# Software pipelining of the head pairs and bf16 masks in a sparse-attention and expert-layer kernel

## The chip, the cores and the metric

The kernel runs on one core of one Trainium2 chip. The metric is device time in microseconds (us) of that core. Engines are named as in the profile: PE (TensorE matmuls), PEld (TensorE weight loads, which overlap PE), DVE (VectorE), ACT (ScalarE), POOL (GpSimd) and SP (the queue that issues transfers).

A single run can be labelled slow when it lies over 1.5% above the fastest of its kernel. Ratios below are the mean time of one kernel's fast runs over the mean of the other's fast runs in the same rounds on the same chip, so a ratio is not quite the ratio of the medians that stand beside it.

## The reference

There are 4 batches of 8 heads with 768 positions of 64 elements. Heads 0, 2 and 6 of each batch are causal. The other five "stream": a query sees the first 4 positions and the last 64. The attention output, as 3072 tokens of 512 elements, goes through an expert layer.

```python
scores = (1.0 / np.sqrt(D)) * np.matmul(q, k.transpose(0, 1, 3, 2))
# causal = rel >= 0;  stream = causal & (is_sink | rel < window)
scores = np.where(mask[None], scores, -1e9)
a = np.exp(scores - np.max(scores, axis=-1, keepdims=True))
a = a / (np.sum(a, axis=-1, keepdims=True) + 1e-09)
x = np.matmul(a, v)            # then (B, H, S, D) -> (B*S, H*D)
h = x @ w_in                   # 512 -> 2048
out = (h / (1.0 + np.exp(-beta * h))) @ w_out   # 2048 -> 512
```

## The kernel before

The first 46 us load and prepare masks and weights. Then come 16 head pairs, two heads (128 rows of data) at a time. The expert stage ends the kernel. For one pair the kernel transposes q and k on TensorE, forms transposed scores block by block for the blocks that the mask leaves, takes the exponential on ScalarE, multiplies by a 0/1 mask on VectorE, and multiplies by V, which carries a column of ones, so that column 64 of the result is the sum of the weights.

```python
# ... pools of the attention stage (bufs = buffers that rotate)
ain bufs=2; aes bufs=3; psp (score PSUM) bufs=4; pou (sum PSUM) bufs=2; ptr (transpose PSUM) bufs=2
for b in range(B):
    for hp in range(0, H, 2):
        # ... load q2, k2, v2; cast to bf16
        for t in range(T):                                  # T = 6
            tpq = ptr.tile([128, 128], BF16, name="tpt")
            nc.tensor.transpose(tpq, q2b[:, t, :, :], ident_bf)
            nc.any.tensor_copy(out=QT2[:, t * 128:(t + 1) * 128], in_=tpq)
            # ... the same for k
        for hh in range(2):
            # ... plan: list of (key block, first and last query block)
            es_all = aes.tile([128, 8, 512], BF16, name="es_all")
            for idx, (kj, ca, cb) in enumerate(plan):
                sp = psp.tile([128, 512], F32, name="sp")
                nc.tensor.matmul(sp[:, 0:w], KT2[po:po + D, ...], QT2[po:po + D, ...])
                nc.scalar.activation(out=esd, in_=sp[:, 0:w], func=Exp, scale=scale)
                # causal head: the diagonal block *= Mc
                # streaming head: esd *= Mstr0[...] (key block 0) or Mstrd[:, 0:w]; masks are fp32
            for qi in range(T):
                pout = pou.tile([128, D + 1], F32, name="pout")
                for j, (idx, kj, cc) in enumerate(contrib):
                    nc.tensor.matmul(pout, es_all[:, idx, ...], V_ext[:, kj, hh, :], ...)
                nc.vector.reciprocal(rec, pout[:, D:D + 1])
                nc.vector.tensor_scalar(out=oqd2[:, qi, hh, :], in0=pout[:, 0:D], scalar1=rec, ...)
        for qi in range(T):
            # ... transpose oqd2 on TensorE (a "tpt" tile again), copy into xT
# ... expert stage: 768 matmuls of 512 columns
```

The order of instructions within each engine is fixed when the program is built, by a list scheduler. `nc.any` lets it choose the engine of a copy. An engine can therefore stand in front of an instruction whose input is not ready: in the kernel before, TensorE stood 36.4 us in front of weighted sums (below).

The softmax here doesn't subtract the row's maximum and nothing guards it: scores larger than these inputs give would overflow.

## Time and profile before

| | before |
|---|---|
| median of 5 runs | 466.07 us (465.95 to 467.4) |
| profiled span | 465.0 us |
| loading, attention, expert stage | to 46, to about 290, to the end |
| time of one causal+streaming pair | 15.75 us |

These lines of the page of the kernel before give each engine's busy time, share of the span and instruction count, then, per engine, the busy share in tenths for 40 equal slices of the span. PEclk is the granted clock of TensorE.

```profile
PE 349.1 (75%) x1844; PEld 160.2 (34%) x1844; DVE 189.0 (41%) x771; ACT 210.8 (45%) x567; POOL 5.4 (1%) x19
...
PE   0000866786677667866786678899999999999996
...
DVE  1094557856767677567756775300000000000000
ACT  0000654565456445644564456552615335272541
...
PEclk9999999999999999999999999999999999999999
```

In the attention, slices 5 to 25, PE shows 6 to 8, DVE mostly 5 to 7, ACT 4 to 6. No engine is full. Soon after, PE is at 9: the expert stage is at TensorE's limit.

This line of the windows view of the kernel before covers attention. After the window and its length, it gives the busy us of PE, PEld, DVE, ACT and POOL with instruction counts, then the granted clock, the DMA share and GB/s.

```profile
46.00:290.00 244.00, 179.18 (x1054) 83.63 (x1055) 165.37 (x715) 137.34 (x443) 0.00 (x0) 1.00 0.35 73
```

Of 244 us PE is busy 179 (73%), DVE 165 (68%), ACT 137 (56%).

These are groups of instructions of the kernel before, each with one shape: line, engine, operation, tiles, shapes and count, then busy us and the mean ns of one, then the engine's idle time before them and what ended it.

```profile
L305 PE MATMUL op<-w_out_sb,gT 128*128 128x512 bf16 x384 | 83.9, 379 | 0.0
L253 PE MATMUL pout<-V_ext,es_all 128*128 128x65 bf16 x552 | 65.7, 241 | 37.5 <-DVE oqd L262 36.4
...
L212 PE MATMUL sp<-QT,KT 64*128 64x512 bf16 x56 | 33.3, 616 | 0.0
...
L241 DVE TENSOR_TENSOR es_all<-es_all,Mstrd 128x256 bf16<-128x256 bf16 x80 | 29.3, 416 | 0.0
...
L229 DVE TENSOR_TENSOR es_all<-es_all,Mc 128x128 bf16<-128x128 bf16 x72 | 17.4, 283 | 0.2
...
L236 DVE TENSOR_TENSOR es_all<-es_all,Mstr 128x512 bf16<-128x512 bf16 x20 | 13.6, 682 | 0.1
```

A 512-column matmul takes 379 ns in the expert stage (L305) and 616 ns as a score matmul (L212). A mask multiply on 256 columns (L241) takes 416 ns.

These lines of the table of waits of the kernel before say who waited for whom, for how many us in total, how often, and the longest wait.

```profile
PEld L253 <- DVE oqd L262: 54.1, 80, 1.9
...
PE pout L253 <- DVE oqd L262: 36.4, 53, 1.8
```

The weighted sums (pout) wait for the scaling (oqd), because the two PSUM banks of the sums come free only when the scaling has read them.

These are pieces of the chain of waits in one pair of the kernel before (start us, length us, what was on the chain).

```profile
98.37 1.60 PE sp L212 x5
...
103.63 0.73 PE pout L253 x11
...
104.39 0.17 DVE rec L261
104.56 0.32 DVE es_all L236
104.88 0.39 DVE oqd L262 x2
105.27 1.54 DVE es_all L241 x5
106.80 0.14 DVE rec L261 x2
106.95 0.26 DVE oqd L262
```

The chain goes through five score matmuls on TensorE, later through eleven sums, and then leaves TensorE: from 104.39 to 107.2 us it lies on VectorE's reciprocals, masks and scalings, and TensorE waits. This line of the page sums the whole chain by engine.

```profile
PE 63%; DVE 23%; issue 6%; ACT 5%; POOL 1%; DMA 1%; SPq 0%; POOLq 0%; ACTq 0%; DVEq 0%
```

VectorE has 23% of the chain though it is never full.

### The profile page before, as it was taken

What the parts mean: (1) busy time and instruction counts of PE and PEld (TensorE: products, weight loads), DVE (VectorE), ACT (ScalarE), POOL (GpSimd) and SP (SyncE); (2) the same over time, 40 slices, a digit from 0 to 9 for tenths busy, and PEclk for the clock granted to TensorE, in tenths of its full rate; (3) what the DMA queues carried; (4) which work ended last, traced back from release to release, by engine and by line L of the source; (5) the groups of instructions that cost most, each with busy time, mean ns of one, the idle gap of its engine ahead of it and who ended that gap; (6) DMA issues with size and microseconds to landing.
All of it is one profiled execution on the core that took longest, in us unless ns stands there. A gap on an engine that the chain in (4) does not pass through costs nothing.

```text
span 465.0 us, 5398 instructions
## 1 busy us (share of the span) xinstructions
PE 349.1 (75%) x1844; PEld 160.2 (34%) x1844; DVE 189.0 (41%) x771; ACT 210.8 (45%) x567; POOL 5.4 (1%) x19
## 2 busy tenths in 40 slices
PE   0000866786677667866786678899999999999996
PEld 0000333333333333333333333344444444444442
DVE  1094557856767677567756775300000000000000
ACT  0000654565456445644564456552615335272541
POOL 2100000000000000000000000000000000000000
PEclk9999999999999999999999999999999999999999
DMA  7916993452332333414310000002011010101101
GB/s 268 397 58 123 200 173 82 89 117 48 83 75 68 87 83 69 103 38 100 68 34 2 0 2 0 1 0 90 1 45 47 23 69 0 68 24 45 47 23 68
DMA packets 83404, 33.91 MB, mean 73 GB/s; under 512 B 77745, under 2 KB 77745, under 8 KB 82865
## 3 DMA queue, kind: packets, MB, share of 16 engines
q1 hardware_dynamic: 83378, 33.58, 28.3%
q8 instruction: 14, 0.23, 0.2%
q14 instruction: 12, 0.10, 0.1%
HBM read 27.28 MB, written 6.29 MB: 72 GB/s over the span
## 4 chain that ended last, share of the span: by engine, by line
PE 63%; DVE 23%; issue 6%; ACT 5%; POOL 1%; DMA 1%; SPq 0%; POOLq 0%; ACTq 0%; DVEq 0%
PE op L305 18%; PE sp L212 12%; PE pout L253 8%; DVE es_all L241 6%; PE tpt L185 5%; DVE oqd L262 5%; ACT KT L186 3%; DVE rec L261 3%; DVE es_all L236 2%; DVE w_in_sb L118 2%; DVE V_ext L175 2%; DVE w_out_sb L126 1%; PE tpt L273 1%; ACT xT L274 1%; DMA q<-in_q_dram 1%
## 5 line engine op out<-in xcount | busy, mean ns | idle before, releaser
L253 PE MATMUL pout<-V_ext,es_all 128*128 128x65 bf16 x552 | 65.7, 241 | 37.5 <-DVE oqd L262 36.4
L220 ACT ACTIVATE es_all<-sp 128x256 bf16<-128x256 f32 (+3 forms) x236 | 85.2, 429 | 18.4 <-PE sp L212 14.0
L305 PE MATMUL op<-w_out_sb,gT 128*128 128x512 bf16 x384 | 83.9, 379 | 0.0
L212 PE MATMUL sp<-QT,KT 64*128 64x256 bf16 (+3 forms) x236 | 78.8, 439 | 0.0
L253 PEld LDWEIGHTS <-es_all 128*128 128x128 bf16 x552 | 38.7, 119 | 86.7 <-DVE oqd L262 54.1
L182 PE MATMUL tpt<-idb,q2b 128*128 128x128 bf16 x96 | 28.5, 297 | 45.8 <-DVE q2b L171 45.5
L274 ACT COPY xT<-tpt 128x128 bf16<-128x128 bf16 x93 | 24.8, 266 | 71.7 <-PE tpt L273 68.4
L290 PEld LDWEIGHTS <-w_in_sb 128*128 128x128 bf16 x384 | 37.9, 99 | 47.2 <-issue 3.9
L305 PEld LDWEIGHTS <-gT 128*128 128x128 bf16 x384 | 37.6, 98 | 45.2
L262 DVE TENSOR_SCALAR oqd<-pout,rec 128x64 bf16<-128x64 f32 x192 | 48.9, 278 | 2.0
L313 ACT COPY osb<-op 128x512 f32<-128x512 f32 x24 | 14.1, 586 | 69.0 <-PE op L305 69.0
L261 DVE RECIPROCAL rec<-pout 128x1 f32<-128x1 f32 x192 | 29.8, 164 | 30.5 <-PE pout L253 27.9
L185 PE MATMUL tpt<-idb,k2b 128*128 128x128 bf16 x96 | 25.9, 270 | 19.0 <-ACT KT L186 11.3
L182 PEld LDWEIGHTS <-q2b 128*128 128x128 bf16 x96 | 10.3, 108 | 70.8 <-issue 70.8
L273 PE MATMUL tpt<-idb,oqd 128*128 128x128 bf16 x96 | 27.3, 289 | 8.2 <-DVE V_ext L176 6.6
L241 DVE TENSOR_TENSOR es_all<-es_all,Mstrd 128x256 bf16<-128x256 bf16 (+1 forms) x100 | 33.3, 390 | 0.0
L212 PEld LDWEIGHTS <-KT 64*128 64x128 bf16 x236 | 22.9, 117 | 27.2 <-issue 17.3
L186 ACT COPY KT<-tpt 128x128 bf16<-128x128 bf16 x79 | 21.1, 267 | 22.2 <-PE tpt L185 22.2
L183 ACT ACT_TABLE_LOAD x1 | 1.3, 1283 | 45.8 <-PE tpt L182 45.8
L236 DVE TENSOR_TENSOR es_all<-es_all,Mstr 128x512 bf16<-128x512 bf16 (+1 forms) x40 | 21.6, 546 | 0.3 <-ACT es_all L220 0.2
L183 DVE COPY QT<-tpt 128x128 bf16<-128x128 bf16 x59 | 13.1, 222 | 17.6 <-PE tpt L182 17.6
L229 DVE TENSOR_TENSOR es_all<-es_all,Mc 128x128 bf16<-128x128 bf16 x72 | 17.4, 283 | 0.2
(231 smaller groups left out, 251.5 us busy)
## 6 DMA issues: line engine op xcount, KB each, us to landing
q<-in_q_dram SPq DMA_DIRECT2D x32, 192.0 KB, 3.3
k<-in_k_dram SPq DMA_DIRECT2D x32, 192.0 KB, 3.4
v<-in_v_dram SPq DMA_DIRECT2D x32, 192.0 KB, 3.0
out_dram<-osb SPq DMA_DIRECT2D x24, 256.0 KB, 2.0
w_in_f<-in_moe_w_in_dram SPq DMA_DIRECT2D x1, 4096.0 KB, 13.2
w_out_f<-in_moe_w_out_dram SPq DMA_DIRECT2D x1, 4096.0 KB, 22.7
beta_row<-in_moe_beta_dram SPq DMA_DIRECT2D x1, 8.0 KB
beta_p<-in_moe_beta_dram SPq DMA_DIRECT2D x1, 8.0 KB, 3.4
```

Source lines behind the costliest of these rows:

```text
L182: nc.tensor.transpose(tpq, q2b[:, t, :, :], ident_bf)
L185: nc.tensor.transpose(tpk, k2b[:, t, :, :], ident_bf)
L186: nc.any.tensor_copy(out=KT2[:, t * 128:(t + 1) * 128], in_=tpk)
L212: nc.tensor.matmul(sp[:, 0:w], KT2[po:po + D, kj * 128:(kj + 1) * 128], QT2[po:po + D, ca * 128:(cb + 1) * 128], start=True, stop=True,)
L220: nc.scalar.activation(out=esd, in_=sp[:, 0:w], func=mybir.ActivationFunctionType.Exp, scale=scale,)
L241: nc.vector.tensor_mul(esd, esd, Mstrd[:, 0:w],)
L253: nc.tensor.matmul(pout, es_all[:, idx, cc * 128:(cc + 1) * 128], V_ext[:, kj, hh, :], start=(j == 0), stop=(j == nci - 1),)
L261: nc.vector.reciprocal(rec, pout[:, D:D + 1])
L262: nc.vector.tensor_scalar(out=oqd2[:, qi, hh, :], in0=pout[:, 0:D], scalar1=rec, scalar2=None, op0=mybir.AluOpType.mult,)
L273: nc.tensor.transpose(tpo, oqd2[:, qi, :, :], ident_bf)
L290: nc.tensor.matmul(hp_, w_in_sb[:, mo, fi * 128:(fi + 1) * 128], xT[:, mo, n0:n0 + NCHUNK], start=(mo == 0), stop=(mo == MO - 1),)
L305: nc.tensor.matmul(op, gT[:, fi, ns * 128:(ns + 1) * 128], w_out_sb[:, fi, :], start=(fi == 0), stop=(fi == FO - 1),)
```

## The change

Its intent is to let the phase of a pair that hangs on VectorE run beside the next pair's transposes and scores, and to make the mask multiplies cheaper. The diff, cut to its core (re-indentation left out):

```diff
+    Mc_b = consts.tile([128, 128], BF16, name="Mc_b")
+    nc.vector.tensor_copy(out=Mc_b, in_=Mc)
+    # ... the same for Mstr0_b (768 columns) and Mstrd_b (256)
@@ pools
-         tc.tile_pool(name="a_in", bufs=2) as ain, \
-         tc.tile_pool(name="a_es", bufs=3) as aes, \
+         tc.tile_pool(name="a_in", bufs=3) as ain, \
+         tc.tile_pool(name="a_es", bufs=2) as aes, \
-         tc.tile_pool(name="a_ps_sp", bufs=4, ...) as psp, \
-         tc.tile_pool(name="a_ps_ou", bufs=2, ...) as pou, \
+         tc.tile_pool(name="a_ps_sp", bufs=3, ...) as psp, \
+         tc.tile_pool(name="a_ps_ou", bufs=3, ...) as pou, \
@@ a pair is split in two
+        def part1(b, hp):   # loads, casts, transposes, scores, exp, masks
+            es_all = aes.tile([128, 2, 8, 512], BF16, name="es_all")   # both heads
-                                    Mc,
+                                Mc_b,
-                                    Mstr0[:, ca * 128:(cb + 1) * 128],
+                                esd, esd, Mstr0_b[:, ca * 128:(cb + 1) * 128]
-                                    esd, esd, Mstrd[:, 0:w],
+                            nc.vector.tensor_mul(esd, esd, Mstrd_b[:, 0:w])
+        def part2(st):      # weighted sums, scaling, output transposes
+        for (b, hp) in pairs:
+            st = part1(b, hp)
+            if pend is not None:
+                part2(pend)
+            pend = st
+        part2(pend)
```

## The prediction

It was written before the changed kernel was built or run.

> **What bounds it now.** The activity rows split the 465.0 us span into loading to 46 us, attention from 46 to about 290, and the expert stage, where TensorE runs at its limit (768 matmuls, 215 ns apart) and nothing changes. So the 244 us of attention count: 16 head pairs, 15.75 us for a causal+streaming pair and 14.8 us for the all-streaming one (start to start of the same burst in the timeline). There TensorE is busy 73%, VectorE 68%, ScalarE 56%: none is full. The chain of waits shows three phases in series per pair: about 4 us of q/k transposes, a ping-pong with the copies out of two PSUM tiles; about 6 us of score matmuls paced by TensorE; about 5.5 us in which VectorE's mask multiplies, reciprocals and scalings hold up the weighted sums (in the table of waits TensorE waits 36 us on the scaling).
>
> TensorE runs at half rate throughout attention: the 512-column score matmul takes 616 ns, the 65-column one 241, while 512 columns take 379 ns in the expert stage. The Trainium skill, "TensorE: Matmul & The Clock Gate", section "Single matmul latency", gives (219+N)/1.2 cold, (398+N)/2.4 warm: 609, 237 and 379 ns; the trace agrees. The granted-clock row (1.00) does not show this gate.
>
> **What the change does.**
> 1. bf16 masks. Mask multiplies take 416 ns (256 wide), 682 (512), 283 (128)[...]. The skill's "VectorE: DVE Perf Modes", "The perf-mode tier table", puts an all-bf16 two-input op at twice that rate. Estimate: 133 ns saved per 256 columns, 80x133 + 20x267 + 20x133 + 92x67 ns = 25 us of VectorE. About 10 us lies on today's chain. Three mask casts are added where VectorE idles 11.6 us: free.
> 2. Software pipelining: transposes, scores and exps of pair i+1 precede the weighted sums of pair i, so the VectorE-bound phase overlaps the next pair's other phases. Nothing is removed.
> 3. Buffers: scores 4 to 3 PSUM banks, sums 2 to 3. Exp needs about 0.36 us per 256-wide tile, the round trip over three banks about 0.9: no new limit.
>
> **The sum.** Per pair afterwards: TensorE, cold, 4.8 (scores) + 2.7 (sums) + 18 transposes at about 0.18 = 10.7 us; VectorE about 9; ScalarE about 8.6. TensorE binds. With 10% lost to fixed instruction orders that mismatch real times: 11.7 us. 16 x 11.7 + 6 us (ends unoverlapped) = 193 us instead of 244: total about 413 us.
>
> **Predicted: 413 us, 8 in 10 between 388 and 440.** Faster by over 2%: 0.9; within 2%: 0.07; slower: 0.03.
>
> **What would show the steps.** Right: 11 to 12.5 us per pair; waits of the sums on the scaling from 36 us to under 12; sums of pair i between score matmuls of pair i+1 in the timeline; 256-wide mask multiply near 280 ns, 512-wide near 415; expert stage unchanged near 171 us; TensorE over 85% busy in attention. Wrong: mask multiplies keep their durations; pairs stay above 14 us.
>
> **What would make it wrong.** Down: if TensorE becomes dense enough to leave its cold state, score matmuls fall to about 380 ns (512 wide) and VectorE at 9 to 10 us a pair binds: about 385 to 390 (I give this 35%). Up: the two transpose tiles are shared by q/k and output transposes; if their order couples the pairs, the overlap is partial: about 435. Or the changed PSUM banks delay the expert stage by a few us.

## The result, and the profile after

| | before | after |
|---|---|---|
| median | 466.16 us (15 runs) | 409.22 us (9 runs, 407.41 to 410.13) |
| ratio of fast runs | | 0.8772 (95%: 0.8757 to 0.8788) |
| profiled span | 465.0 us | 407.4 us |
| attention | 46 to about 290 us | 46 to about 235 us |
| one causal+streaming pair, from first score matmul to first score matmul | 15.75 us | about 12.0 us (10.9 for two streaming heads) |
| copies out of the transpose tiles on ACT / DVE | 209 / 79 | 258 / 30 |

The result is correct and 57 us faster. The lines of the page of the kernel after that answer to those above:

```profile
PE 339.7 (83%) x1844; PEld 158.9 (39%) x1844; DVE 154.1 (38%) x725; ACT 219.0 (54%) x616; POOL 5.5 (1%) x19
...
PE   0000398899898999898999999999999999999996
...
DVE  0268267767777767766667710000000000000000
ACT  0000477777778777877777665164262461541731
...
PEclk9999999999999999999999999999999999999999
```

From the sixth slice on PE reads 8 or 9, through attention and expert stage alike; the long stretch of 6 to 8 is gone. The windows view of the kernel after, for attention:

```profile
46.00:235.00 189.00, 171.06 (x1073) 82.97 (x1073) 133.34 (x685) 145.29 (x491) 0.00 (x0) 1.00 0.47 94
```

Of 189 us PE is busy 171 (90%), DVE 133 (71%), ACT 145 (77%). PE's busy time fell by 8 us only, so most of the gain is idle time that was filled: 65 us idle before, 18 after. Per pair (one sixteenth) that is 10.7 us of PE, 8.3 of DVE and 9.1 of ACT.

The groups of the kernel after, each with one shape:

```profile
L324 PE MATMUL op<-w_out_sb,gT 128*128 128x512 bf16 x384 | 83.9, 379 | 0.0
L266 PE MATMUL pout<-V_ext,es_all 128*128 128x65 bf16 x552 | 69.9, 247 | 2.8 <-DVE oqd L275 2.6
...
L222 PE MATMUL sp<-QT,KT 64*128 64x512 bf16 x56 | 34.1, 609 | 0.3 <-ACT es_all L230 0.3
...
L250 DVE TENSOR_TENSOR es_all<-es_all,Mstrd_b 128x256 bf16<-128x256 bf16 x80 | 22.6, 290 | 6.3 <-ACT es_all L230 5.4
...
L239 DVE TENSOR_TENSOR es_all<-es_all,Mc_b 128x128 bf16<-128x128 bf16 x72 | 15.5, 220 | 7.5 <-ACT es_all L230 6.8
...
L246 DVE TENSOR_TENSOR es_all<-es_all,Mstr_b 128x512 bf16<-128x512 bf16 x20 | 8.4, 419 | 2.3 <-ACT es_all L230 2.3
```

The masks fell from 416 to 290 ns (256 columns), 682 to 419 (512) and 283 to 220 (128). The step from 256 to 512 columns costs (419-290)/256 = 0.50 ns a column, before (682-416)/256 = 1.04. A fixed part of 150 to 160 ns stays. That is what the Trainium skill, "VectorE: DVE Perf Modes", section "The perf-mode tier table", says of a two-input operation whose operands are all bf16: the rate per element doubles. The trace agrees on the rate, and the short tiles get less than half off because of the fixed part. Score matmuls stay at 609 ns. The table of waits of the kernel after:

```profile
PEld L266 <- DVE oqd L275: 16.4, 38, 1.0
...
PE pout L266 <- DVE oqd L275: 2.6, 6, 0.8
```

The sums' wait on the scaling fell from 36.4 to 2.6 us, that of their weight loads from 54.1 to 16.4. The chain of the kernel after, by engine:

```profile
PE 76%; ACT 8%; issue 6%; DVE 6%; POOL 1%; DMA 1%; SPq 1%; POOLq 0%; ACTq 0%; DVEq 0%
```

VectorE's part fell from 23 to 6%, PE's rose from 63 to 76%, and ScalarE's from 5 to 8%. The timeline of PE in the kernel after shows why (start us, length us, engine, line, operation, tiles, shapes, count):

```profile
109.48 1.14 PE L222 MATMUL sp<-QT,KT 64*128 64x512 bf16 x3
...
110.55 0.51 PE L266 MATMUL pout<-V_ext,es_all 128*128 128x65 bf16 x6
...
110.88 0.30 PE L285 MATMUL tpt<-idb,oqd 128*128 128x128 bf16 x1
...
111.10 0.28 PE L222 MATMUL sp<-QT,KT 64*128 64x128 bf16 x1
...
111.60 1.03 PE L222 MATMUL sp<-QT,KT 64*128 64x512 bf16 x3
```

Between score matmuls of the new pair (L222) stand sums of the pair before (L266) and its output transposes (L285). While VectorE scales one sum, TensorE has other work.

The expert stage did not change. It ran from 235.7 to 407.4 us after (172 us), and from 290.3 to 465.0 before (175 us), where its first 7 us were shared with sums and transposes of the last pair.

### The profile page after: what moved, and what is told of

The parts are those of the page before. It is cut to its first block, busy times and chain, and to the rows that moved or that the text cites. A ratio compares the mean times of both kernels' runs of the same rounds, so it can differ in the third digit from the quotient of the medians.

```text
span 407.4 us, 5398 instructions
## 1 busy us (share of the span) xinstructions
PE 339.7 (83%) x1844; PEld 158.9 (39%) x1844; DVE 154.1 (38%) x725; ACT 219.0 (54%) x616; POOL 5.5 (1%) x19
## 4 chain that ended last, share of the span: by engine, by line
PE 76%; ACT 8%; issue 6%; DVE 6%; POOL 1%; DMA 1%; SPq 1%; POOLq 0%; ACTq 0%; DVEq 0%
PE op L324 20%; PE sp L222 17%; PE pout L266 8%; ACT es_all L230 4%; PE tpt L208 3%; PE tpt L205 3%; PE tpt L285 3%; DVE w_in_sb L125 2%; DVE w_out_sb L133 1%; ACT QT L206 1%; ACT xT L286 1%; ACT KT L209 1%; DMA v<-in_v_dram 1%; DVE es_all L250 1%; DVE oqd L275 1%
## 5 line engine op out<-in xcount | busy, mean ns | idle before, releaser
L230 ACT ACTIVATE es_all<-sp 128x256 bf16<-128x256 f32 (+3 forms) x236 | 88.2, 420 | 24.3 <-PE sp L222 20.8
L222 PE MATMUL sp<-QT,KT 64*128 64x256 bf16 (+3 forms) x236 | 83.2, 437 | 0.6 <-ACT es_all L230 0.3
L266 PE MATMUL pout<-V_ext,es_all 128*128 128x65 bf16 x552 | 69.9, 247 | 2.8 <-DVE oqd L275 2.6
L205 PE MATMUL tpt<-idb,q2b 128*128 128x128 bf16 x96 | 26.4, 275 | 48.7 <-DVE q2b L194 45.4
L266 PEld LDWEIGHTS <-es_all 128*128 128x128 bf16 x552 | 45.5, 126 | 46.9 <-DVE oqd L275 16.4
L222 PEld LDWEIGHTS <-KT 64*128 64x128 bf16 x236 | 21.2, 111 | 26.6 <-issue 13.5
L205 PEld LDWEIGHTS <-q2b 128*128 128x128 bf16 x96 | 11.7, 121 | 50.5 <-issue 48.6
L285 PE MATMUL tpt<-idb,oqd 128*128 128x128 bf16 x96 | 25.4, 287 | 6.1 <-ACT xT L286 5.0
L250 DVE TENSOR_TENSOR es_all<-es_all,Mstrd_b 128x256 bf16<-128x256 bf16 (+1 forms) x100 | 25.5, 276 | 6.4 <-ACT es_all L230 5.4
L206 ACT COPY QT<-tpt 128x128 bf16<-128x128 bf16 x91 | 24.2, 267 | 5.2 <-PE tpt L205 1.8
L286 ACT COPY xT<-tpt 128x128 bf16<-128x128 bf16 x80 | 19.2, 277 | 6.1 <-PE tpt L285 5.7
L239 DVE TENSOR_TENSOR es_all<-es_all,Mc_b 128x128 bf16<-128x128 bf16 x72 | 15.5, 220 | 7.5 <-ACT es_all L230 6.8
L285 PEld LDWEIGHTS <-oqd 128*128 128x128 bf16 x96 | 10.9, 118 | 16.2 <-issue 11.2
```

The lines of the kernel that those rows point to most:

```text
L222: nc.tensor.matmul(sp[:, 0:w], KT2[po:po + D, kj * 128:(kj + 1) * 128], QT2[po:po + D, ca * 128:(cb + 1) * 128], start=True, stop=True,)
L230: nc.scalar.activation(out=esd, in_=sp[:, 0:w], func=mybir.ActivationFunctionType.Exp, scale=scale,)
L250: nc.vector.tensor_mul(esd, esd, Mstrd_b[:, 0:w])
L266: nc.tensor.matmul(pout, es_all[:, hh, idx, cc * 128:(cc + 1) * 128], V_ext[:, kj, hh, :], start=(j == 0), stop=(j == nci - 1),)
L285: nc.tensor.transpose(tpo, oqd2[:, qi, :, :], ident_bf)
```

## The experiments

The theory, from the prediction, is A: overlap makes most of the gain, the masks give a smaller part, and afterwards TensorE, in its slow state, binds a pair. Its rivals: B, the masks carry most of the gain; C, the buffers do; D, after the change the latency of the chain score, exp, mask, sum binds rather than TensorE's work. W is about the clock: if TensorE could be kept in its fast state, attention would get shorter still. The expectations refer to these by letter or in words. Every kernel here gave a correct result.

### Masks alone, overlap alone, buffers alone

The first takes the kernel after and gives it back its fp32 masks.

```diff
-    Mc_b = ...; Mstr0_b = ...; Mstrd_b = ...      # the three casts
-                                Mc_b,
+                                Mc,
-                                esd, esd, Mstr0_b[:, ca * 128:(cb + 1) * 128]
+                                esd, esd, Mstr0[:, ca * 128:(cb + 1) * 128]
-                            nc.vector.tensor_mul(esd, esd, Mstrd_b[:, 0:w])
+                            nc.vector.tensor_mul(esd, esd, Mstrd[:, 0:w])
```

> The changed kernel with the masks left in fp32, everything else as changed. Theory A (overlap: after the change the cold TensorE sets the pair time at about 10.7 of 11.8 us, VectorE has slack): mask multiplies return to about 416 and 682 ns, VectorE gains back about 23 us of busy time, but the total rises by at most 8 us, to 409 to 417. Rival B (relief of VectorE is what made the gain): most of the 23 us comes back, 425 to 435.

It took 422.72 us (0.9067, 0.9035 to 0.9099). The waits of the sums on the scaling in this kernel:

```profile
PEld L259 <- DVE oqd L268: 20.7, 31, 2.3
...
PE pout L259 <- DVE oqd L268: 8.4, 8, 1.9
```

They lie well below 54.1 and 36.4 us, so the overlap works without the new masks. But 13.5 us over the kernel after, for 19.6 us more VectorE busy time (173.7 against 154.1 us), is more than "VectorE has slack" allowed (at most 8 us), and less than B asked. A missed expectation. My reading: a mask multiply stands between the exponential and the sum of its tile, so its duration can be felt there though VectorE has idle time elsewhere; no run here separates that from the amount of VectorE work (see the run with extra VectorE copies below).

The second takes the kernel before and gives it the bf16 masks only.

```diff
+    # the three casts
-                                    Mc,
+                                    Mc_b,
-                                    Mstr0[:, ca * 128:(cb + 1) * 128],
+                                    Mstr0_b[:, ca * 128:(cb + 1) * 128],
-                                    esd, esd, Mstrd[:, 0:w],
+                                    esd, esd, Mstrd_b[:, 0:w],
```

> The kernel before with bf16 masks and nothing else changed. Theory A: only the mask time on the serial chain is saved, about 10 us: 452 to 460. Rival B: VectorE's waits shrink throughout, 430 to 440.

It took 448.29 us (0.9616), 18 us less than before. Both the theory (10 us) and the rival that gives the masks most of the gain missed, on opposite sides. The same waits in this kernel:

```profile
PEld L260 <- DVE oqd L269: 39.9, 64, 1.4
...
PE pout L260 <- DVE oqd L269: 27.3, 49, 1.2
```

TensorE still waits on the scaling, 27.3 us of the 36.4. Cheaper masks shorten the VectorE phase; they do not hide it. But nearly all that they save counts there: VectorE's busy time fell by 22.8 us (189.0 to 166.2), the time by 18. On the page of this kernel VectorE has 17% of the chain, 76 us of 448, where it had 23%, 107 us of 465.

The third changes the kernel before in its buffers only: `a_in` 2 to 3, score banks 4 to 3, sum banks 2 to 3.

```diff
-         tc.tile_pool(name="a_in", bufs=2) as ain, \
+         tc.tile_pool(name="a_in", bufs=3) as ain, \
-         tc.tile_pool(name="a_ps_sp", bufs=4, ...) as psp, \
-         tc.tile_pool(name="a_ps_ou", bufs=2, ...) as pou, \
+         tc.tile_pool(name="a_ps_sp", bufs=3, ...) as psp, \
+         tc.tile_pool(name="a_ps_ou", bufs=3, ...) as pou, \
```

> The kernel before with the new buffer counts alone (inputs 3, score banks 3, sum banks 3). Theory A: the same within 2%, 460 to 470, since the phases of a pair stay in series. Rival C (the third sum bank lets TensorE run ahead of the scaling, and that made the gain): below 445.

It took 461.5 us (0.9895): 1% less, as A expected.

The fourth takes the kernel after with the old buffer counts (the reverse edit, except `a_es`, which stays 2 because each tile now holds two heads).

> The changed kernel with the old buffer counts (inputs 2, score banks 4, sum banks 2). Theory A: most of the gain stays, 409 to 422; the waits of the sums on the scaling grow. Rival C: the gain is mostly lost, above 435.

It took 413.18 us (0.8851), 4 us more than after, in A's range; the sums' wait on the scaling grew from 2.6 to 6.4 us. Both say the same: the buffers are worth 4 to 5 us, so C falls.

With 466.2 us as the time before, the masks alone are worth 18 us and the overlap with its buffers 43.5. Their sum is 61, together they gave 57. The two parts overlap by 4 us only. Whichever is counted first, the overlap is 39 to 43.5 us of the 57, about 69 to 76%.

### What binds the kernel after

Five kernels start from the kernel after. One reorders the score matmuls, three add work to one engine each, and one changes how often TensorE must wait for a copy.

```diff
# score matmuls of the two heads in turn instead of one head after the other
-            for hh in range(2):
-                for idx, (kj, ca, cb) in enumerate(plan):
+            for idx in range(max(len(p) for p in plans)):
+                for hh in range(2):
```

> The changed kernel, with the score matmuls of the two heads of a pair issued in turn (head 0 reads partitions 0 to 63, head 1 partitions 64 to 127). [...]Theory A (the cold TensorE sets the pair time): with alternating halves of the array the weight load, and perhaps the matmul itself, overlaps; [...]385 to 400 us, until ScalarE (about 9 us a pair) takes over. Rival D (no engine binds after the change; the pair time is a latency chain through exp, mask, sum, scaling and copy): less than 8 us, 401 to 410.

It took 406.33 us (0.8722), 3 us less than after: short of A's 385 to 400, in the range of D. The scheduler did not keep the order strictly. Where one score matmul directly follows another, 36 of 87 start within 10 ns of the one before in this trace, as against 2 of 103 in the kernel after, where neighbours of 256 columns start 0.17 to 0.21 us apart. So matmuls of two heads in different rows of the array can start almost together. As the profile models the ends of matmuls, how much of their time overlaps stays open; the time of the kernel hardly felt it.

```diff
# more TensorE work: before each accumulation of sums, its first matmul twice more
+                    for _ in range(2):
+                        nc.tensor.matmul(pout, es_all[:, hh, idx0, cc0 * 128:(cc0 + 1) * 128],
+                                         V_ext[:, kj0, hh, :], start=True, stop=True)
```

> The changed kernel with two extra TensorE instructions per weighted sum (its first matmul issued twice more beforehand and overwritten, result unchanged): 384 more at 0.066 us, about 25 us of TensorE work. Theory A: nearly all shows, 428 to 436. Rival D: about half or less, 412 to 422.

It took 417.62 us (0.8969), 8.4 us more than after. Eleven such matmuls took 0.73 us in the chain above, 66 ns each, so 384 of them are some 25 us of work (an estimate). That is the range of D. But the run is not clean, as the granted-clock row of its page shows:

```profile
PEclk9999999999655557655556569999999999999999
```

TensorE turned to its fast state three times within attention, at 100.2, 161.7 and 223.1 us, for 6.8, 6.8 and 3.4 us, 17 us together, and each time fell back to 5 (the 0.50 of the record). Extra work made some windows dense enough, and those windows paid back part of it. So this run does not refute A by itself.

```diff
# more VectorE work: one copy of 128 columns per sum
+                    junk = asm.tile([128, 128], BF16, name="junk")
+                    nc.vector.tensor_copy(out=junk, in_=ident_bf)
# more ScalarE work (another kernel): one copy of 32 columns per sum of the first head
+                    if hh == 0:
+                        nc.scalar.copy(out=junk, in_=ident_bf[:, 0:32])
```

> The changed kernel with one extra 128-column bf16 copy on VectorE per weighted sum, that nothing waits for: 192 at about 0.13 us, about 25 us of VectorE work. Theory A as predicted (VectorE has slack): under 8 us, 409 to 417. After the fp32-mask run (+13.5 us for 23 us of VectorE work) I expect rather 10 to 16 us, 419 to 425, which would say that VectorE's time counts too (rival D or a shared bound).

> The changed kernel with an extra 32-column copy on ScalarE for every weighted sum of the first head, that nothing waits for: 96 at about 0.2 us, about 20 us of ScalarE work. Theory A: under 5 us, 409 to 414. Rival D: 8 to 15 us, 417 to 424.

```profile
L274 DVE COPY junk<-idb 128x128 bf16<-128x128 bf16 x192 | 25.9, 184 | 0.1
```

```profile
L275 ACT COPY junk<-idb 128x32 bf16<-128x32 bf16 x96 | 13.6, 217 | 0.0
```

The copies on VectorE (first line) cost 6.3 us (415.55, 0.8918): in A's range, and less than the 10 to 16 us that was expected. The copies on ScalarE (second line) cost nothing (408.47, 0.8769), which speaks against D at first sight.

But neither run loads attention as was meant. Nothing waits for a copy, and the scheduler put most of them early. In the traces 79 of the 96 ScalarE copies begin before 60 us and all before 90, so this run says nothing of ScalarE's slack in the rest of attention. Of the 192 VectorE copies 109 begin before 60 us, 13 from there to the last output transpose of the tenth pair, and 70 in the last six pairs. The early ones delayed the first transpose from 45.4 to 48.3 us, about 3 of the 6.3 us. The last six pairs test the slack: with 70 copies, some 13 us of VectorE work, the stretch from that transpose to the first expert matmul took 64.2 us, as against 62.7 in the kernel after. So 13 us of such work cost about 1.5 us there, in one profile each. With fp32 masks the same stretch took 64.8 us, only 2.1 more; most of their 13.5 us fell on earlier pairs. The runs therefore show slack on VectorE for work that nothing waits for, but not that the place of the mask work, rather than its amount, made it cost 13.5 us. D is neither shown nor refuted by these two runs.

```diff
# three transposes share one PSUM tile and one copy of 384 columns (q, k and output)
-            for t in range(T):
-                tpq = ptr.tile([128, 128], BF16, name="tpt")
-                nc.tensor.transpose(tpq, q2b[:, t, :, :], ident_bf)
-                nc.any.tensor_copy(out=QT2[:, t * 128:(t + 1) * 128], in_=tpq)
+            for t in range(0, T, 3):
+                tpq = ptr.tile([128, 3, 128], BF16, name="tpt")
+                for u in range(3):
+                    nc.tensor.transpose(tpq[:, u, :], q2b[:, t + u, :, :], ident_bf)
+                nc.any.tensor_copy(out=QT2[:, t * 128:(t + 3) * 128], in_=tpq)
```

> The changed kernel with three 128x128 transposes written into one PSUM tile and copied out by one 384-column copy: 288 copies become 96. Estimate from the exp of 384 columns on ScalarE (0.51 us) and the 128-column copy (0.267 us): ScalarE and VectorE save about 2 us of copy time a pair. Theory A (TensorE sets the pair time, but waits on ScalarE's copies and exps for about a fifth of the chain): the copy waits go, 393 to 402. Rival (a tile of three must be full before it is copied, so the chain gets no shorter): 404 to 412.

It took 398.95 us (0.8559), 10 us less than after, in A's range. One group of the copies on ScalarE, in the kernel after and in this one:

```profile
L206 ACT COPY QT<-tpt 128x128 bf16<-128x128 bf16 x91 | 24.2, 267 | 5.2 <-PE tpt L205 1.8
```

```profile
L207 ACT COPY QT<-tpt 128x384 bf16<-128x384 bf16 x31 | 14.9, 482 | 8.7 <-PE tpt L206 7.6 <-PE pout L268 0.8
```

One copy of 384 columns takes about 480 ns in place of three of 267, and there are 96 copies instead of 288. ScalarE's busy time fell from 219.0 to 199.7 us. The number of TensorE instructions is the same and its score matmuls are as slow as before (611 ns), so TensorE's own work had not been the whole bound: the transposes had waited for their copies. Whether the fewer hand-overs or the 19 us less of ScalarE work made the gain stays open: the run with extra ScalarE copies can't tell, as its copies ran before most of attention, and no other run separates the two.

### The clock of TensorE

The score matmuls of the kernel after take 609 ns in attention though PE is busy 90%. This kernel puts a useless matmul of 128 rows and 512 columns before each accumulation of sums; the sums then overwrite its bank.

```diff
-                    pout = pou.tile([128, D + 1], F32, name="pout")
+                    pout_full = pou.tile([128, 512], F32, name="pout")
+                    nc.tensor.matmul(pout_full, w_in_sb[:, 0, 0:128], w_in_sb[:, 1, 0:512],
+                                     start=True, stop=True)
+                    pout = pout_full[:, 0:D + 1]
```

> The changed kernel with one useless 128x512 matmul in front of every weighted sum, into the sum's own PSUM bank and overwritten by it (result unchanged): 192 matmuls, 0.427 us each at the cold clock, 0.215 us at the warm one. In the run with 384 extra small matmuls the array turned fast (64x512 matmul in well under 0.5 us) in three stretches of 4 to 6 us. Theory W (the clock follows how densely TensorE works, and attention stays cold because it is not dense enough): the array turns fast for most of attention, real TensorE work shrinks from about 10.9 to about 6.7 us a pair, fillers add 2.6, the pair time falls to 9.5 to 11 us and the total to 375 to 400. Theory K (attention's own instructions, 64-row matmuls and transposes, keep the array cold whatever the density): the fillers cost 12 x 0.427 = 5.1 us a pair less the present idle time, total 450 to 485.

It took 400.38 us (0.8578), 8.8 us less than after, with 192 more matmuls: just above the 375 to 400 that W expected, and far below the 450 to 485 of K, which falls. Its groups and its granted-clock row:

```profile
L264 PE MATMUL pout<-w_in_sb 128*128 128x512 bf16 x192 | 79.1, 420 | 31.9 <-DVE w_in_sb L125 29.5 <-DVE oqd L283 2.4
L274 PE MATMUL pout<-V_ext,es_all 128*128 128x65 bf16 x552 | 62.1, 204 | 0.0
...
L222 PE MATMUL sp<-QT,KT 64*128 64x512 bf16 x56 | 23.5, 420 | 0.0
```

```profile
PEclk9999999989998999989899999999999999999999
```

The mean of the 512-column score matmuls fell from 609 to 420 ns. It is a mixture: 611 ns before 75 us, 382 ns for the 14 of them between 86 and 126 us. From 75.2 us on the record shows the fast state except for single stretches of 3.41 us.

The row needs care. In this kernel it prints 9 for the slices before 75 us too, where the matmuls take 611 ns. In the trace of the kernel after the first clock record stands at 239.8 us, and the row prints 9 and the windows view 1.00 from the start. Before its first change the record says nothing; the durations do. The profile models the ends of matmuls, but their starts tell the same: in the pre-warming kernel below, the first 14 of 16 useless 512-column matmuls start 0.40 to 0.43 us apart (mostly 0.427), and the last two, after the recorded change, 0.215 to 0.217.

The next kernel has both edits, packing (the diff of the section above) and filler (the diff just above), together:

> The changed kernel with both edits that gained: transposes three to a tile and copy, and the useless 128x512 matmul before every sum. If the two gains are separate (ScalarE copy waits; the array's clock) they add to about 19 us and the total is 385 to 393. If the packed version leaves TensorE with more gaps, so that the array cools down again, the gain is that of one alone or less: 396 to 405, with 64x512 score matmuls back near 600 ns.

It took 393.06 us in the median (390.64, 391.14 and 394.98 us fast, 396.58 slow; ratio of the fast ones 0.8412, 0.8364 to 0.8461). This is the fastest kernel, about 4% below the kernel after by the ratios of fast runs (0.8412 against 0.8772). It stands at the edge of the 385 to 393 that were expected if the two gains add. It spreads more than the others. In its profiled run, the slow one, TensorE was slow until 88 us, and fast afterwards.

The last kernel tries to begin attention in the fast state: 16 useless matmuls before the first pair, added to the kernel just above.

```diff
+        warm = psp.tile([128, 512], F32, name="sp")
+        for i in range(16):
+            nc.tensor.matmul(warm, w_out_sb[:, FO - 1, 0:128], w_out_sb[:, i, :], start=True, stop=True)
```

> The packed and filled kernel with 16 useless 128x512 matmuls on the finished weights just before attention, when TensorE is otherwise idle (they can start at about 39 us, when the weights are done, and need about 7 us). In the profiled run of the packed and filled kernel the array was at the slow clock from 46 to 88 us, with TensorE busy over 93% of that time, so some 4 pairs ran slow with fillers on top. If the clock follows recent density, attention now starts fast and the total is 378 to 387. If the first pairs cool it down again at once, or the warm-up delays the first pair, 389 to 397.

It took 396.99 us (0.8504, 0.8469 to 0.854), no better than without them, as the second branch expected (389 to 397). From its timeline, the warming matmuls, and from its windows view, two stretches of attention:

```profile
40.14 6.31 PE L304 MATMUL sp<-w_out_sb 128*128 128x512 bf16 x16 [9.31 <-DVE w_out_sb L133]
```

```profile
52.40:86.50 34.10, 32.09 (x168) 13.89 (x168) 20.32 (x95) 18.98 (x49) 0.00 (x0) 0.50 0.81 152
86.50:220.00 133.50, 122.82 (x1007) 61.83 (x1005) 108.07 (x533) 95.39 (x252) 0.00 (x0) 0.96 0.40 86
```

The warming worked: the record shows the fast state from about 45.6 us, and the last of the 16 matmuls takes 379 ns. It then stays fast until 52.4 us and falls to 0.50 until 86.5, where PE is busy 32.1 of 34.1 us. From 86.5 on it is mostly fast (0.96), as without the warming. In the two windows of 3.41 us before it fell, columns streamed for 38 and 35% of the time (worked out as below).

**What the changes of state go with.** In these traces the state changes only at multiples of 3.413 us from one another, which is the window that the Trainium skill gives in "TensorE: Matmul & The Clock Gate", Part 1. I cut five traces (after, more TensorE work, filler, packing with filler, pre-warming) into these windows and worked out, for each, the share of it in which columns stream: columns divided by 1.2 or 2.4 per ns, by the state (512 columns in 0.427 or 0.215 us, as above), a matmul of 64 rows counted half. There are 297 windows, from about 42 us to the first windows of the expert stage. One matmul that has a weight load in the trace but no record of its own (at 245.3 us, with more TensorE work) is counted.

| window | windows | share, rows counted | next state |
|---|---|---|---|
| slow | 135 | 0.09 to 0.76 (one above 0.75) | slow |
| slow | 17 | 0.75 to 1.00 | fast |
| fast | 13 | 0.27 to 0.36 | slow |
| fast | 132 | 0.36 to 1.00 | fast |

So TensorE turned fast after a window at about 0.75 or more and slow after one at 0.36 or less. One slow window at or above the lowest that turned fast stayed slow. If rows are not counted, 20 do (lowest 0.79). If rows are counted but transposes left out, 32 do (lowest 0.44). The kernel after lay between 0.25 and 0.68 throughout attention: its busy engine spends much of its time in score matmuls of 64 rows and between instructions. This is a pattern found in the traces afterwards. No run isolated the 64 rows or the transposes, so what the monitor counts stays open.

## Why the prediction was right, and where it was not

The total was right: 413 us against 409.22, in the range of 388 to 440, and the branch was the one given most weight.

1. **Three phases in series, overlap removes the wait.** Right. Waits on the scaling 36.4 to 2.6 us (expected under 12), VectorE's part of the chain 23 to 6%, sums between score matmuls in the timeline, and a pipelined kernel with the old masks at 422.72 us.
2. **TensorE 10.7 us a pair, VectorE 9, ScalarE 8.6, plus 10%: 11.7 us.** Measured 10.7, 8.3, 9.1 and 12.0 for a causal+streaming pair, 10.9 for a streaming one, 11.6 on the mean. Attention took 189 us, as against 193 predicted. The closeness is in part luck: the 10% was a guess, and no run shows that fixed orders are its reason. Nor are 10.7 us of busy time 10.7 us of streaming: the columns of a pair alone need 7.5 us in the slow state (an estimate: 143400 columns in attention, 512 in 0.427 us, 16 pairs).
3. **Masks near 280 and 415 ns.** Measured 290 and 419. But "About 10 us lies on today's chain" was too small: alone they gave 18 us. VectorE's busy time fell by 22.8 us there and its part of the chain by 31 us, while TensorE's grew. The 10 us of the prediction were a share of mask work on today's chain, but in phases that run in series nearly all of the saving counted. In the pipelined kernel they still gave 13.5.
4. **"TensorE binds."** In part. It is 90% busy, but 13.5 us came from masks that only VectorE carries, 10 us from fewer copies, and some 25 us of extra TensorE work cost 8.4, in a run that its fast windows blur. Chain latency still counts, 8% of it on ScalarE and 6% on VectorE. The Trainium skill, "Perfetto Trace Analysis", section "Identifying the Most-Contended Engine", warns that the busy share of matmuls is no good measure of how near TensorE is to its limit; this agrees, 90% busy and 10 us to be had by packing copies. The page's reason, that pipelined instructions look smaller in a trace, isn't what is seen here: the busy share says too much, as columns need 7.5 of the 10.7 us.
5. **Buffers: no new limit.** Right; they helped by 4 to 5 us.
6. **35% for TensorE leaving its slow state.** It did not, in the kernel after (609 ns). The filler matmuls show that the branch is real and what it needed, and that it was worth less than I had put on it: 400.4 us with 192 matmuls thrown in.
7. **"The granted-clock row (1.00) does not show this gate."** Half right. It does show it from the first change in the trace on; before that the row is blank paper that prints as 1.00.

## What to carry to other kernels

When a phase of a loop body waits on a second engine, issue the next iteration's work for the first engine ahead of it: that gave about 69 to 76% of the 57 us here, with no instruction less. An engine that is far from full can still cost time after that: 20 us of mask work on VectorE, 71% busy, cost 13.5, and packing three small evacuations of PSUM into one gave 10. When you add work to test an engine's slack, look in the trace where the scheduler put it before you read the time. Read the state of TensorE from the durations and starts of matmuls of known size, not from a busy share or a clock row. In these traces it turned fast only after windows in which columns streamed 75% of the time or more, rows counted.

## What the Trainium skill lacked or had wrong

- "TensorE: Matmul & The Clock Gate", Part 1, lets the clock fall after an idle window, and also tells of a kernel in which short idle gaps between groups of matmuls were enough; it gives no share for either. Here it fell after windows in which columns streamed for 27 to 36% of the time (rows counted), with no idle window, and rose only after windows of 75% or more. A matmul stage that is 90% busy can stay slow throughout (609 ns for 512 columns).
- The same page, Part 4, has transposes not counting as busy for the clock in the same way. In these traces the changes of state separate well only if the transposes are counted (1 of 135 slow windows out of place, 32 without); worked out from traces, not isolated.
- The same page advises padding a thin operand; it does not say that wholly useless matmuls can pay: 192 of them took the time from 409.2 to 400.4 us. Nor that warming ahead of a thin stretch is lost: the fast state ended 6.8 us after it began, at 52.4 us.
- The same page, "Seeing it yourself", reads the state from the recorded changes and warns that they can be unreliable. It does not say that there is none before the first change, so that a view can print 1.00 over matmuls of 609 ns (first record at 239.8 us in the kernel after).
- No page has the cost of small PSUM evacuations side by side ("Perfetto Trace Analysis" comes nearest, with a fixed overhead per operation and the advice to group operations): 267 ns for 128 columns and 480 for 384 on ScalarE; packing three in one gave 10 us.
